# Gated mix of an S4 convolution and a GeGLU: another form of the block convolution, and a shorter gelu, last tile and mix in the feed-forward part

## Chip, cores and metric

The kernel runs on one core of one Trainium2 chip. The metric is the device time of one execution in microseconds (us), lower is better. A profile is one further execution recorded by the hardware profiler; "span" is what it covers, from the first to the last recorded instruction.

## What is computed

The input x is 2048 tokens of 640 channels in bf16. A state-space layer gives every channel a filter of 2048 taps, and the causal convolution of x with it is one branch; a GeGLU feed-forward layer is the other. A gate per token mixes them.

```
K[d,l] = Re( sum_n C[d,n] * exp(dt[d]*A[d,n]*l) * dt[d]*B[d,n] )        # 640 x 2048, n = 128
a = causal_conv(x, K) + x * Dskip                                        # over the 2048 tokens
b = ( gelu_tanh(x @ w_gate) * (x @ w_up) ) @ w_down                      # 640 -> 1728 -> 640
g = sigmoid( sum(x * gate_w) )                                           # one number per token
out = g * a + (1 - g) * b
```

## The kernel before, in words

The program runs in four stages, one after the other in the source. The instructions of each engine stand in an order that the framework's scheduler makes from the source order and the dependencies; buffers are taken from pools, and a pool that is opened after another one was closed lies on the same memory, so that its first writers wait for the last users of the old one.

1. *Filter generation* (lines 103 to 314). For ten blocks of 64 channels it makes tables of exponentials and sines and contracts them on PE. The result K_sb holds the filter with 128 tokens on the partitions. The change leaves this stage as it is.

2. *Convolution* (lines 321 to 426). The 2048 tokens are cut into four blocks of 512 (NB = 4), and the transform has length T = 1024. All four blocks of x are loaded at once into u_sb, which is a_sb itself (L332). Half-integer frequencies need 512 real and 512 imaginary parts and no special Nyquist row, so that a spectrum is two parts (q) of four tiles (ft) of 128 frequencies. The tables FK, FU and FI are made in twelve wide steps: two tensor_scalar operations make the phase as an integer whose lower 16 bits wrap by themselves (L357), and one Sin takes 1024 columns at once (L359). fwd_block (L364) transforms a block: 64 matmuls of 320 columns, each group of eight evicted by a Scalar copy (L375). The filter's blocks get another table than the input's, and combine (L377) joins neighbouring filter blocks beforehand, so that the product of spectra needs no correction for wrap-around later. products(c) (L385) multiplies and adds spectra on Vector with operations 2560 columns wide. inverse(c) (L402) transforms back on PE, 16 matmuls per output tile of 128 tokens, and adds x * Dskip while it evicts (L412, L413).

3. *Gate and up projections* (L441 to L494). x is loaded again, transposed (xT, five transposing loads), then the weights Wg, Wu, Wd and the gate vector gwc, all from SP's queue. The gate logits are 80 small matmuls into a PSUM tile of their own (L458). Then there are 14 hidden tiles (13 of 128 and one of 64) times four stretches of 512 tokens. For each, five matmuls make the gate part pGt and five the up part pUt. Scalar copies both to bf16 (Gs, Us); Vector builds the gelu's polynomial in three operations, Scalar takes a sigmoid, and Vector multiplies twice (L484 to L494). The result is HT.

4. *Down projection and mix* (L496 to L513). For each of 16 tiles of 128 tokens 28 matmuls (14 of 512 and 14 of 128 columns) fill pD, which has one buffer. Scalar copies it to b_sb, Vector subtracts and mixes in two operations, and SP stores the tile.

Lines that the steps of the prediction touch: L338 to L360 (tables), L364 to L375 (forward), L377 to L383 (combine), L385 to L400 (products), L402 to L416 (inverse), L443 to L453 (loads of the feed-forward part), L455 to L462 (gate), L474 to L494 (gate and up), L497 to L513 (down).

Of the kernel before, what the change touches and what calls it, by code (L numbers as in the profile page):

```python
# [9 lines left out]
ALU = mybir.AluOpType  # L10
ACT = mybir.ActivationFunctionType
FP32 = mybir.dt.float32
BF16 = mybir.dt.bfloat16
I32 = mybir.dt.int32
# [8 lines left out]
def kernel(  # L23
# [19 lines left out]
    nc = tc.nc  # L43
# [279 lines left out]
    with ExitStack() as k2:  # L323
        big = k2.enter_context(tc.tile_pool(name="spec", bufs=1))
        wk = k2.enter_context(tc.tile_pool(name="cwork", bufs=2))
        psT = k2.enter_context(tc.tile_pool(name="pstf", bufs=2, space=bass.MemoryType.PSUM))
        psY = k2.enter_context(tc.tile_pool(name="psinv", bufs=2, space=bass.MemoryType.PSUM))
        DH = D // 2
        NF = 4
        I16 = mybir.dt.int16  # L330

        u_sb = a_sb  # L332
        for c in range(NB):
            nc.sync.dma_start(out=u_sb[:, 4 * c:4 * c + 4, :],
                              in_=u2[c * S:(c + 1) * S, :].rearrange("(t p) d -> p t d", p=128))

        odd_i = big.tile([128, 512], I32, name="odd_i")
        nc.gpsimd.iota(odd_i[:], pattern=[[2, 512]], base=1, channel_multiplier=0)  # L338
        oddf = big.tile([128, 512], FP32, name="oddf")
        nc.vector.tensor_copy(out=oddf[:], in_=odd_i[:])  # L340
        FU = big.tile([128, 4, 2, 512], BF16, name="FU")
        FK = big.tile([128, 4, 2, 512], BF16, name="FK")
        FI = big.tile([128, NF, 2, 512], BF16, name="FI")
        scl = big.tile([128, 12], FP32, name="scl")
        for a in range(4):
            nc.vector.tensor_scalar(out=scl[:, a:a + 1], in0=row_f[:], scalar1=32.0, scalar2=16.0 * (256 * a + 1),
                                    op0=ALU.mult, op1=ALU.add)
            nc.vector.tensor_scalar(out=scl[:, 4 + a:5 + a], in0=row_f[:], scalar1=32.0, scalar2=32.0 * 128 * a,
                                    op0=ALU.mult, op1=ALU.add)
            f0 = 256 * (a // 2) + a % 2  # L350
            nc.vector.tensor_scalar(out=scl[:, 8 + a:9 + a], in0=row_f[:], scalar1=64.0, scalar2=16.0 * (2 * f0 + 1),
                                    op0=ALU.mult, op1=ALU.add)
        for tab, s0 in ((FK, 4), (FU, 0), (FI, 8)):
            for a in range(4):
                ph = wk.tile([128, 2, 512], I32, name="ph")
                for q in range(2):
                    nc.vector.tensor_scalar(out=ph[:, q, :], in0=oddf[:], scalar1=scl[:, s0 + a:s0 + a + 1],  # L357
                                            scalar2=(16384.0 if q == 0 else 0.0), op0=ALU.mult, op1=ALU.add)
                nc.scalar.activation(out=tab[:, a, :, :], in_=ph[:].bitcast(I16)[:, :, 0:1024:2], func=ACT.Sin,  # L359
                                     scale=TWO_PI * FUDGE / 65536.0)  # L360

        Uf = big.tile([128, NB, 2, NF, D], BF16, name="Uf")
        Kf = big.tile([128, NB, 2, NF, D], BF16, name="Kf")

        def fwd_block(tab, src, b, spec):
            for ft in range(NF):
                f0 = 256 * (ft // 2) + ft % 2
                for q in range(2):
                    pU = psT.tile([128, 2, 512], FP32, name="pU")
                    for h in range(2):  # L370
                        for k in range(4):
                            nc.tensor.matmul(pU[:, h, 0:DH], lhsT=tab[:, k, q, f0:min(512, f0 + 256):2],  # L372
                                             rhs=src[:, 4 * b + k, h * DH:(h + 1) * DH],
                                             start=(k == 0), stop=(k == 3))
                    nc.scalar.copy(out=spec[:, b, q, ft, :].rearrange("p (h d) -> p h d", h=2), in_=pU[:, :, 0:DH])  # L375

        def combine(m):  # L377
            for ft in range(NF):
                odd = ft % 2 == 1
                nc.vector.tensor_tensor(out=Kf[:, m, 0, ft, :], in0=Kf[:, m, 0, ft, :], in1=Kf[:, m - 1, 1, ft, :],  # L380
                                        op=(ALU.subtract if odd else ALU.add))
                nc.vector.tensor_tensor(out=Kf[:, m, 1, ft, :], in0=Kf[:, m, 1, ft, :], in1=Kf[:, m - 1, 0, ft, :],
                                        op=(ALU.add if odd else ALU.subtract))  # L383

        def products(c):  # L385
            M = wk.tile([128, 2, NF, D], BF16, name="M")
            for i in range(c + 1):
                Ur, Ui = Uf[:, i, 0, :, :], Uf[:, i, 1, :, :]
                Kr, Ki = Kf[:, c - i, 0, :, :], Kf[:, c - i, 1, :, :]
                for q, (k0, k1, op1) in enumerate(((Kr, Ki, ALU.subtract), (Ki, Kr, ALU.add))):  # L390
                    if i == 0:
                        nc.vector.tensor_tensor(out=M[:, q], in0=Ur, in1=k0, op=ALU.mult)
                    else:
                        t0 = wk.tile([128, NF, D], BF16, name="t0")
                        nc.vector.tensor_tensor(out=t0[:], in0=Ur, in1=k0, op=ALU.mult)
                        nc.vector.tensor_tensor(out=M[:, q], in0=M[:, q], in1=t0[:], op=ALU.add)  # L396
                    t1 = wk.tile([128, NF, D], BF16, name="t1")
                    nc.vector.tensor_tensor(out=t1[:], in0=Ui, in1=k1, op=ALU.mult)
                    nc.vector.tensor_tensor(out=M[:, q], in0=M[:, q], in1=t1[:], op=op1)  # L399
            return M  # L400

        def inverse(c, M):  # L402
            for mo in range(4):
                pY = psY.tile([128, 2, 512], FP32, name="pY")
                for h in range(2):
                    for q in range(2):
                        for ft in range(NF):
                            nc.tensor.matmul(pY[:, h, 0:DH], lhsT=FI[:, ft, q, 128 * mo:128 * mo + 128],  # L408
                                             rhs=M[:, q, ft, h * DH:(h + 1) * DH],
                                             start=(q == 0 and ft == 0), stop=(q == 1 and ft == NF - 1))  # L410
                t = 4 * c + mo
                nc.vector.tensor_tensor(out=u_sb[:, t, :], in0=u_sb[:, t, :], in1=dsk[:], op=ALU.mult)  # L412
                nc.vector.scalar_tensor_tensor(out=a_sb[:, t, :].rearrange("p (h d) -> p h d", h=2),  # L413
                                               in0=pY[:, :, 0:DH], scalar=2.0 / T,
                                               in1=u_sb[:, t, :].rearrange("p (h d) -> p h d", h=2),
                                               op0=ALU.mult, op1=ALU.add)  # L416

        for b in range(NB):
            fwd_block(FK, K_sb, b, Kf)
        for c in range(NB):  # L420
            fwd_block(FU, u_sb, c, Uf)
        for m in range(NB - 1, 0, -1):
            combine(m)
        for c in range(NB):
            M = products(c)
            inverse(c, M)
# [3 lines left out]
    dchs = [(0, 512), (512, D - 512)]  # L430
    with ExitStack() as k3:
# [3 lines left out]
        psC = k3.enter_context(tc.tile_pool(name="psconst", bufs=1, space=bass.MemoryType.PSUM))  # L435
# [19 lines left out]
        pG = psC.tile([128, TC], FP32, name="pgate")  # L455
# [5 lines left out]
        nc.scalar.copy(out=glog[:], in_=pG[:])  # L461
# [5 lines left out]

        HT = fp.tile([128, nft, L], BF16, name="HT")
        GELU_C = 2.0 * math.sqrt(2.0 / math.pi)
        for ft in range(nft):  # L470
            fsz = 128 if ft < nft_full else f_last
            f0 = ft * 128
            for tq in range(L // 512):
                toks = slice(tq * 512, (tq + 1) * 512)  # L474
                pGt = psF.tile([128, 512], FP32, name="pGt")
                pUt = psF.tile([128, 512], FP32, name="pUt")
                for kt in range(nkt):
                    nc.tensor.matmul(pGt[:fsz, :], lhsT=Wg[:, kt, f0:f0 + fsz], rhs=xT[:, kt, toks],  # L478
                                     start=(kt == 0), stop=(kt == nkt - 1))
                for kt in range(nkt):  # L480
                    nc.tensor.matmul(pUt[:fsz, :], lhsT=Wu[:, kt, f0:f0 + fsz], rhs=xT[:, kt, toks],  # L481
                                     start=(kt == 0), stop=(kt == nkt - 1))
# [13 lines left out]
        for tt in range(TC):  # L496
# [9 lines left out]
            if "b" in dbg:  # L506
                nc.sync.dma_start(out=dbg["b"][toks, :], in_=b_sb[:])
# [37 lines left out]
```

## Time and profile before

| | us |
|---|---|
| median of 3 runs (776.99 to 779.27) | 777.49 |
| the profiled execution, its own time | 777.49 |
| its span | 775.7 |
| PE busy (64% of the span) | 494.7 |
| Vector busy (75%) | 579.3 |
| Scalar busy (58%) | 446.6 |
| GpSimd busy (1%) | 6.3 |

"PE" is the matrix engine and "PEld" its weight loads, DVE is Vector, ACT Scalar, POOL GpSimd, and SP the engine that issues the loads and stores. The page cuts the span into 40 equal slices of 19.4 us and gives the busy share of each in tenths; these rows show the stages one after the other:

```profile
PE   0036656566658556435899963306199999998886
...
DVE  5978899889998998866157999994068787773333
ACT  1129999999999999984766400000077766751111
...
PEclk9999697798698689666999995757599999999999
```

The first 18 slices are filter generation (Scalar and Vector near full), then come the transforms (PE), the products (Vector alone), one slice and a bit with no engine at work, the gate and up projections and the down projection (PE). "PEclk" is the PE clock that was granted, in tenths of full speed. In the rows of groups that are quoted further down, the numbers behind the bar are total busy us, mean ns of one, and the idle time of the engine just before with what ended it. In timelines the columns are start and length in us, engine, line, operation, and in brackets the idle time before it and its releaser.

### The profile page before, as it was taken

To read this page: it belongs to the slowest core of one execution; us is meant where nothing else is said; L and a number is where in the kernel's file an instruction comes from. 1 tells how busy PE (TensorE), PEld (TensorE's weight loads), DVE (VectorE), ACT (ScalarE), POOL (GpSimd) and SP (SyncE) were. 2 spreads that over 40 slices of the span, in tenths; PEclk is the share of its full clock that TensorE was granted. 3 is DMA by queue.
4 is the path that set the end of the run, shared out by engine and by line. 5 is a ranking of instruction groups with operands and counts; after the bars stand their busy time and mean duration, and the time that the engine had idled before them with its cause. 6 is when DMAs were issued, how large, how long until landed. Compare 5 with 4: busy or idle time off the path is not lost.

```text
span 775.7 us, 8859 instructions
## 1 busy us (share of the span) xinstructions
PE 494.7 (64%) x3518; PEld 259.9 (34%) x3556; DVE 579.3 (75%) x906; ACT 446.6 (58%) x492; POOL 6.3 (1%) x26
## 2 busy tenths in 40 slices
PE   0036656566658556435899963306199999998886
PEld 0012223233224222133577641203044444444443
DVE  5978899889998998866157999994068787773333
ACT  1129999999999999984766400000077766751111
POOL 2000000000000000000000000000000000000000
PEclk9999697798698689666999995757599999999999
DMA  3000000000000000060000000001940000000000
GB/s 68 0 0 0 1 1 15 0 14 14 1 15 14 1 14 14 0 164 14 1 1 1 2 0 0 1 0 33 282 165 1 1 0 1 1 10 26 35 35 35
DMA packets 44650, 19.01 MB, mean 25 GB/s; under 512 B 37248, under 2 KB 43328, under 8 KB 44608
## 3 DMA queue, kind: packets, MB, share of 16 engines
q1 hardware_dynamic: 44608, 18.44, 9.4%
q8 instruction: 28, 0.46, 0.3%
q14 instruction: 14, 0.11, 0.1%
HBM read 9.91 MB, written 2.62 MB: 16 GB/s over the span
## 4 chain that ended last, share of the span: by engine, by line
ACT 40%; DVE 31%; PE 23%; SPq 3%; issue 2%; DMA 2%; ACTq 0%; DVEq 0%
PE pD L502 8%; PE pU L372 5%; ACT sg L492 4%; DVE M L399 3%; DVE sg L493 3%; DVE q L490 3%; DVE M L396 2%; DVE HT L494 2%; PE pY L408 2%; SPq L443 2%; ACT L249 2%; DVE q L488 2%; ACT L266 1%; ACT b_sb L505 1%; DVE q L489 1%
## 5 line engine op out<-in xcount | busy, mean ns | idle before, releaser
L484 ACT CAST Gs<-pGt 128x512 bf16<-128x512 f32 (+1 forms) x56 | 32.3, 577 | 124.8 <-PE pGt L478 124.4
L257 DVE TENSOR_SCALAR kM<-pph 128x512 f32<-128x512 f32 x120 | 79.6, 682 | 22.3 <-PE pph L253 14.5
L478 PE MATMUL pGt<-xT,Wg 128*128 128x512 bf16 (+1 forms) x269 | 69.8, 384 | 25.2 <-DMA Wg<-in_B_w_gate_dram 22.1
L408 PE MATMUL pY<-M,FI 128*128 128x320 bf16 x256 | 42.1, 329 | 57.5 <-DVE M L399 55.1
L502 PE MATMUL pD<-Wd,HT 128*128 128x128 bf16 (+3 forms) x440 | 68.0, 298 | 12.8 <-ACT b_sb L505 12.4
L481 PE MATMUL pUt<-xT,Wu 128*128 128x512 bf16 (+1 forms) x280 | 69.2, 379 | 0.4 <-ACT Us L486 0.4
L492 ACT ACTIVATE sg<-q 128x512 bf16<-128x512 bf16 (+1 forms) x56 | 35.2, 630 | 35.6 <-DVE q L490 35.3
L408 PEld LDWEIGHTS <-FI 128*128 128x128 bf16 x256 | 27.1, 106 | 72.3 <-DVE M L399 51.2
L509 DVE TENSOR_TENSOR diff<-a_sb,b_sb 128x640 f32<-128x640 bf16 x16 | 13.2, 825 | 50.1 <-ACT b_sb L505 50.1
L502 PEld LDWEIGHTS <-HT 128*128 128x128 bf16 x448 | 34.8, 97 | 46.3 <-issue 22.0
L505 ACT CAST b_sb<-pD 128x640 bf16<-128x640 f32 x16 | 11.0, 691 | 66.1 <-PE pD L502 66.1
L478 PEld LDWEIGHTS <-Wg 128*128 128x128 bf16 (+1 forms) x280 | 27.6, 99 | 60.3 <-issue 30.2
L372 PE MATMUL pU<-K_sb,FK 128*128 128x320 bf16 x256 | 38.8, 313 | 11.7 <-ACT FK L359 8.8
L488 DVE TENSOR_TENSOR q<-Gs 128x512 bf16<-128x512 bf16 (+1 forms) x56 | 23.4, 418 | 26.6 <-ACT Gs L484 26.6
L493 DVE TENSOR_TENSOR sg<-sg,Gs 128x512 bf16<-128x512 bf16 (+1 forms) x56 | 23.8, 424 | 21.1 <-ACT sg L492 20.4
L481 PEld LDWEIGHTS <-Wu 128*128 128x128 bf16 (+1 forms) x280 | 27.6, 99 | 33.4 <-issue 0.7
L253 PE MATMUL pph<-RX_1_104,b_bf 128*128 128x512 bf16 x40 | 19.1, 486 | 29.7 <-DVE p_2486 L258 7.3
L253 PE MATMUL pph<-RX_0_103,b_bf 128*128 128x512 bf16 x40 | 17.3, 437 | 30.7 <-DVE p_1655 L258 6.4
L372 PE MATMUL pU<-a_sb,FU 128*128 128x320 bf16 x256 | 34.9, 299 | 0.0
L372 PEld LDWEIGHTS <-FK 128*128 128x128 bf16 x256 | 25.5, 101 | 24.8 <-ACT FK L359 10.7
L486 ACT CAST Us<-pUt 128x512 bf16<-128x512 f32 (+1 forms) x56 | 32.5, 582 | 1.3 <-PE pUt L481 1.3
L375 ACT CAST Uf<-pU 128x640 bf16<-128x640 f32 x32 | 22.1, 692 | 12.6 <-PE pU L372 12.6
(383 smaller groups left out, 1219.5 us busy)
## 6 DMA issues: line engine op xcount, KB each, us to landing
a_sb<-in_A_u_dram SPq DMA_DIRECT2D x4, 640.0 KB, 5.5
out_dram<-o_sb SPq DMA_DIRECT2D x16, 160.0 KB, 1.8
Wg<-in_B_w_gate_dram SPq DMA_DIRECT2D x1, 2160.0 KB, 8.7
Wu<-in_B_w_up_dram SPq DMA_DIRECT2D x1, 2160.0 KB, 13.5
Wd<-in_B_w_down_dram SPq DMA_DIRECT2D x1, 2080.0 KB, 19.5
K_sb<-K_671 SPq DMA_DIRECT2D x4, 64.0 KB, 2.3
K_sb<-K_948 SPq DMA_DIRECT2D x4, 64.0 KB, 2.5
K_sb<-K_1225 SPq DMA_DIRECT2D x4, 64.0 KB, 2.2
```

The costliest lines, as they stand in the source:

```text
L253: nc.tensor.matmul(pph[:], lhsT=lhs_b, rhs=rhs_rx, start=True, stop=True)
L257: nc.vector.tensor_scalar(out=kM[:], in0=tau_src, scalar1=MAGIC, scalar2=None, op0=ALU.add)
L372: nc.tensor.matmul(pU[:, h, 0:DH], lhsT=tab[:, k, q, f0:min(512, f0 + 256):2], rhs=src[:, 4 * b + k, h * DH:(h + 1) * DH], start=(k == 0), ...
L408: nc.tensor.matmul(pY[:, h, 0:DH], lhsT=FI[:, ft, q, 128 * mo:128 * mo + 128], rhs=M[:, q, ft, h * DH:(h + 1) * DH], start=(q == 0 and ft ...
L478: nc.tensor.matmul(pGt[:fsz, :], lhsT=Wg[:, kt, f0:f0 + fsz], rhs=xT[:, kt, toks], start=(kt == 0), stop=(kt == nkt - 1))
L481: nc.tensor.matmul(pUt[:fsz, :], lhsT=Wu[:, kt, f0:f0 + fsz], rhs=xT[:, kt, toks], start=(kt == 0), stop=(kt == nkt - 1))
L484: nc.scalar.copy(out=Gs[:fsz], in_=pGt[:fsz])
L486: nc.scalar.copy(out=Us[:fsz], in_=pUt[:fsz])
L488: nc.vector.tensor_tensor(out=q[:fsz], in0=Gs[:fsz], in1=Gs[:fsz], op=ALU.mult)
L492: nc.scalar.activation(out=sg[:fsz], in_=q[:fsz], func=ACT.Sigmoid, scale=GELU_C)
L493: nc.vector.tensor_tensor(out=sg[:fsz], in0=sg[:fsz], in1=Gs[:fsz], op=ALU.mult)
L502: nc.tensor.matmul(pD[:, d0:d0 + dn], lhsT=HT[:fsz, ft, toks], rhs=Wd[:fsz, ft, d0:d0 + dn], start=(ft == 0), stop=(ft == nft - 1))
```

## The change

Both halves of the program behind filter generation are exchanged.

*Convolution.* The half-integer form gives way to one with whole frequencies 0 to 512: nine tiles of 128 rows (NT = 9), real and imaginary parts in turn, the ninth holding only the Nyquist row. One forward table FW serves filter and input. FW and FI are built in 72 tiles of 128x128: each takes six or seven Vector operations, with the phase reduced to the nearest whole turn by adding and subtracting a large constant, and a Sin. The input is loaded block by block into ub, a pool of two buffers that is opened after the tables' work pool was closed; x * Dskip is put into a_sb beforehand. The products are operations on single tiles of 640 columns. There is no combine; a step Mc = Sc + sgn * Sprev joins the sums of two successive blocks instead. The transforms' matmuls are split at 512 columns: 512 and 128.

*Feed-forward part.* The gelu is one Scalar function read straight from PSUM, and one Vector operation multiplies it with the up part in PSUM. The last half tiles of gate and up share one group of matmuls through a joined weight tile Wl, which GpSimd copies together. The gate logits use a buffer of pGt. pD has two halves of 320 columns and two buffers; Scalar forms g * a ahead of time (ga), and one Vector operation adds (1 - g) * pD.

The diff, cut to its core:

```diff
+        FW = big.tile([128, 4, NT, 128], BF16, name="FW")
+        FI = big.tile([128, NT, 4, 128], BF16, name="FI")
...
+        dw = dctx.enter_context(tc.tile_pool(name="dftwork", bufs=2))
+
+        def angle_negfrac(dst_pt, v_in, shape):
...
+            nc.vector.tensor_scalar(out=tv, in0=v_in, scalar1=1.0 / T, scalar2=None, op0=ALU.mult)
...
+            nc.vector.tensor_scalar(out=kv, in0=tv, scalar1=MAGIC, scalar2=None, op0=ALU.add)
+            nc.vector.scalar_tensor_tensor(out=dst_pt, in0=kv, scalar=-MAGIC, in1=tv, op0=ALU.add, op1=ALU.subtract)
+
+        for kind in range(2):
+            for a in range(4):
...
+                for mt in range(NT):
+                    dst = FW[:, a, mt, :] if kind == 0 else FI[:, mt, a, :]
...
+                    if kind == 0:
+                        nc.vector.tensor_scalar(out=fv[:], in0=col_f[:], scalar1=float(128 * tt), scalar2=None, op0=ALU.add)
+                        nc.vector.tensor_tensor(out=v[:], in0=fv[:], in1=s_val[:].to_broadcast([128, 128]), op=ALU.mult)
...
+                    nc.vector.tensor_scalar(out=v[:], in0=v[:], scalar1=off, scalar2=None, op0=ALU.add)
+                    nfq = dw.tile([128, 128], FP32, name="nfq")
+                    angle_negfrac(nfq[:], v[:], [128, 128])
+                    if kind == 0:
+                        nc.scalar.activation(out=dst, in_=nfq[:], func=ACT.Sin, scale=sin_scale)
+                    else:
+                        tmp = dw.tile([128, 128], FP32, name="sinv")
+                        nc.scalar.activation(out=tmp[:], in_=nfq[:], func=ACT.Sin, scale=sin_scale)
+                        nc.vector.tensor_scalar(out=dst, in0=tmp[:], scalar1=2.0 / T, scalar2=None, op0=ALU.mult)
...
+        def fwd_block(src, kidx, spec, b):
+            for mt in range(NT):
+                pU = psT.tile([128, D], FP32, name="pU")
+                for (d0, dn) in dchs:
+                    for k in range(4):
+                        nc.tensor.matmul(pU[:, d0:d0 + dn], lhsT=FW[:, k, mt, :], rhs=src[:, kidx(k), d0:d0 + dn],
+                                         start=(k == 0), stop=(k == 3))
+                nc.scalar.copy(out=spec[:, b, mt, :], in_=pU[:])
...
+            ub = upool.tile([128, 4, D], BF16, name="ub")
+            nc.sync.dma_start(out=ub[:], in_=u2[c * S:(c + 1) * S, :].rearrange("(t p) d -> p t d", p=128))
+            for k in range(4):
+                nc.vector.tensor_tensor(out=a_sb[:, 4 * c + k, :], in0=ub[:, k, :], in1=dsk[:], op=ALU.mult)
+            fwd_block(ub, lambda k: k, Uf, c)
...
+                        nc.vector.tensor_tensor(out=tmp[:], in0=Ur, in1=Kr, op=ALU.mult)
+                        nc.vector.tensor_tensor(out=Sr, in0=Sr, in1=tmp[:], op=ALU.add)
...
+                    nc.vector.scalar_tensor_tensor(out=Mc[:, mt, :], in0=Sprev[:, mt, :],
+                                                   scalar=sgn[:], in1=Sc[:, mt, :],
+                                                   op0=ALU.mult, op1=ALU.add)
...
+                    for kt in range(NT):
+                        nc.tensor.matmul(pY[:, d0:d0 + dn], lhsT=FI[:, kt, mo, :], rhs=Mc[:, kt, d0:d0 + dn],
+                                         start=(kt == 0), stop=(kt == NT - 1))
+                tcx = 4 * c + mo
+                nc.vector.tensor_tensor(out=a_sb[:, tcx, :], in0=a_sb[:, tcx, :], in1=pY[:], op=ALU.add)
...
-        pG = psC.tile([128, TC], FP32, name="pgate")
+        pG = psF.tile([128, 512], FP32, name="pGt")
...
-                nc.scalar.copy(out=Gs[:fsz], in_=pGt[:fsz])
...
-                nc.scalar.copy(out=Us[:fsz], in_=pUt[:fsz])
...
-                nc.scalar.activation(out=sg[:fsz], in_=q[:fsz], func=ACT.Sigmoid, scale=GELU_C)
...
+                    nc.scalar.activation(out=Gs[:], in_=pGt[:], func=ACT.Gelu_apprx_tanh)
+                    nc.vector.tensor_tensor(out=HT[:, ft, toks], in0=pUt[:], in1=Gs[:], op=ALU.mult)
+                else:
+                    for kt in range(nkt):
+                        nc.tensor.matmul(pGt[:], lhsT=Wl[:, kt, :], rhs=xT[:, kt, toks],
+                                         start=(kt == 0), stop=(kt == nkt - 1))
...
-            pD = psF.tile([128, D], FP32, name="pD", bufs=1)
...
+            nc.scalar.activation(out=ga[:], in_=a_sb[:, tt, :], func=ACT.Copy, scale=gf[:, tt:tt + 1])
+            pD = psD.tile([128, 2, 512], FP32, name="pD")
+            for h in range(2):
...
-            nc.scalar.copy(out=b_sb[:], in_=pD[:])
...
-            nc.vector.tensor_tensor(out=diff[:], in0=a_sb[:, tt, :], in1=b_sb[:], op=ALU.subtract)
...
+            nc.vector.scalar_tensor_tensor(out=o_sb[:].rearrange("p (h d) -> p h d", h=2), in0=pD[:, :, 0:DH],
+                                           scalar=omg[:, tt:tt + 1],
+                                           in1=ga[:].rearrange("p (h d) -> p h d", h=2),
                                            op0=ALU.mult, op1=ALU.add)
```

## The prediction

> **What bounds the kernel now.** I first read the busy times of stretches that I cut at the stage borders (columns: PE, weight loads, Vector, Scalar, GpSimd busy, granted PE clock, DMA share, GB/s), then the timeline at the borders and in one period of each loop, then the rows of single groups for prices.
>
> ```profile
> 354.90:404.00 49.10, 38.61 (x256) 25.58 (x257) 18.13 (x54) 32.64 (x43) 0.00 (x0) 0.90 0.04 6
> 412.50:538.50 126.00, 68.36 (x451) 45.92 (x449) 118.93 (x104) 17.33 (x26) 0.00 (x0) 0.77 0.00 0
> 538.50:560.40 21.90, 0.00 (x0) 0.00 (x0) 0.71 (x1) 0.00 (x0) 0.00 (x0) 0.60 0.95 241
> 560.40:689.70 129.30, 125.68 (x630) 57.33 (x641) 99.76 (x270) 89.29 (x167) 0.00 (x0) 0.99 0.09 32
> 689.70:775.70 86.00, 68.00 (x441) 34.75 (x448) 31.11 (x43) 13.31 (x21) 0.00 (x0) 1.00 0.09 31
> ```
>
> Filter generation ends on Vector at 354.9. Tables and the transform of K follow (PE), then the products until 538.5 (Vector busy 119 of 126 us), a pure load, gate and up matmuls (PE 126 of 129), and the down projection (PE 68 of 86).
>
> ```profile
> 515.42 1.49 DVE L395 TENSOR_TENSOR t_4142<-Uf,Kf 128x2560 bf16<-128x2560 bf16 x1
> 516.82 1.49 DVE L399 TENSOR_TENSOR M<-M,t_4139 128x2560 bf16<-128x2560 bf16 x1
> ...
> 528.58 9.76 PE L408 MATMUL pY<-M,FI 128*128 128x320 bf16 x56 [2.29 <-DVE M L399]
> 538.38 0.82 DVE L413 SCALAR_TENSOR_TENSOR a_sb<-pY,a_sb 128x640 bf16<-128x640 f32 x1 [1.35 <-PE pY L408]
> 538.49 13.00 SPq L443 DMA_TRANSPOSE xT<-in_A_u_dram  x5
> ```
>
> Wide products start every 1.40 us though each lasts 1.49, also where one needs the result of the op before last: neighbours overlap by 0.09. The load of xT starts when the last inverse transform ends.
>
> ```profile
> 601.18 1.24 PE L478 MATMUL pGt<-xT,Wg 128*128 128x512 bf16 x5
> 602.26 1.24 PE L481 MATMUL pUt<-xT,Wu 128*128 128x512 bf16 x5
> ...
> 705.02 4.28 PE L502 MATMUL pD<-Wd,HT 128*128 128x512 bf16 x28 [0.82 <-ACT b_sb L505]
> 709.37 0.69 ACT L505 CAST b_sb<-pD 128x640 bf16<-128x640 f32 x1 [4.41 <-PE pD L502]
> 710.12 4.28 PE L502 MATMUL pD<-Wd,HT 128*128 128x512 bf16 x27 [0.82 <-ACT b_sb L505]
> ```
>
> Five matmuls of 512 columns take 1.08 us, 0.216 each, without a break: gate and up stand at PE's pace, the gelu chain is hidden. Down is not: a tile takes 5.10 us, PE waits for the eviction of its only pD.
>
> ```profile
> L380 DVE TENSOR_TENSOR Kf<-Kf 128x640 bf16<-128x640 bf16 x12 | 5.3, 487 | 24.9 <-ACT Kf L375 24.9
> 27.57 0.82 DVE L162 TENSOR_TENSOR r_149<-vr 128x640 f32<-128x640 f32 x1
> 43.24 0.49 DVE L181 TENSOR_SCALAR u2t<-u2t 128x640 f32<-128x640 f32 x1
> 355.18 0.13 DVE L346 TENSOR_SCALAR scl<-row_f 128x1 f32<-128x1 f32 x1
> ```
>
> These are the prices for the new small Vector operations.
>
> **What the Trainium skill says.** "VectorE: DVE Perf Modes", section "The perf-mode tier table": tensor_tensor runs at 2x in bf16 and 1x in fp32, tensor_scalar at 2x in fp32. The trace agrees: 487 ns against 820 at 640 elements, and 490 for the fp32 tensor_scalar. The table has no row for scalar_tensor_tensor. Same page, section on the TRN2 errata: each SBUF-source instruction pays a fixed extra, so many small tiles pay it often; here 4 x 0.403 = 1.61 us for what one 1.40 us operation did. "TensorE: Matmul & The Clock Gate", Part 1: after about 3.4 us idle the array runs at half clock until as long busy. Agrees: after the 22 us load, five matmuls took 2.5 us (0.43 apart) before 0.216. "ScalarE: Activation LUTs", "What ACT_TABLE_LOAD costs": all functions cost the same per element, so gelu from PSUM should cost what the copy Gs does (577 ns); a load is given at 1283 ns, and the trace has 1283.
>
> **Tables and K transform** (354.9 to 404 now). Twelve wide Sin calls go. Vector gets 476 operations for FW and FI. A 128x128 fp32 tensor_scalar: 0.13 + 128/640 x (0.49 - 0.13) = 0.20 us, 0.13 apart with overlap; tensor_tensor or scalar_tensor_tensor likewise 0.28, 0.20 apart. The built program's order interleaves two tiles, so each needs the op before last, as in the products. Unlike there the operations are short; bounds: 0.13/0.20 apart, or full duration plus the 0.04 seen between dependent ones (0.24/0.32). I take the lower. An FW tile: 4 x 0.13 + 2 x 0.20 = 0.92; 32 of them and some 2 us of small ones: 31.4, to 386.3. FI adds a tiny one per tile: 32 x 0.99 + 4 = 35.7, to 422. None of it precedes 354.9: in the order all of it stands behind the last K0 copy, and up to there both programs are alike on PE, Vector and Scalar.
>
> PE's first group needs FW of all four k: 354.9 + 0.75 x 31.4 + 2 + 0.3 (Sin) = 380.7. A group is 4 x 0.216 plus four of 128 columns at (4.28 - 0.15 - 14 x 0.216)/14 = 0.08: 1.18. 36 groups are 42.5, cold start 2, to 425. Scalar holds the evictions (0.69) and FI's Sins in one order; each can wait for the other, 3 us more: 428. The loads of ub wait for FI's last Vector and Scalar instruction (their buffers lie where the work tiles were), though they are issued on SP with nothing else behind but each other. They land 5.5 us later (as a_sb now): 433.5. Two cold groups and an eviction, 4.4 + 0.7: products can start at 438.6, against 412.6 now.
>
> **Products.** Removed: 72 wide operations x 1.40 = 101 us; the combines were hidden behind PE. Added: 304 of 128x640, (487 ns less the 0.085 overlap = 0.403) = 122.5; 27 Mc steps, bounds 0.403 (2x) and 0.737 (1x, as L413, which however reads PSUM), taken at 0.737 = 19.9; 16 additions from pY at 0.737 = 11.8, as many as now; 8 of the u x dsk multiplies (the other 8 stand ahead) 3.2. Sum 157.4, less the last four additions behind the tail: 154.5. Behind Mc of c = 0, 1, 2 Vector waits about 1, 1 and 2 us for the first inverse; what is queued behind these waits is the next block's products. PE's own work, 36 more forward groups (42.5) and 16 inverse tiles of 18 x 0.148 = 2.66, is 85 of these 160 us and hidden. Vector's last Mc: 438.6 + 154.5 + 4 = 597.1. Two interleaved inverses end 1.9 later, two more 5.3, cold clock 2: xT's load can start at 606.3 instead of 538.5: **+67.8**.
>
> **Gate and up.** Load and landings keep their distances. In the order PE now does only 10 pUt matmuls, then the 80 gate ones, which need gwc, the last load; it landed 34.4 us behind xT's first issue (572.9). Now PE had done 52 matmuls by then. So from 576.1 (old clock) 560 - 20 merged - 10 = 530 x 0.216 = 114.5 remain, to 690.6; gelu's two table loads hold up the third pGt 1.5, cold start 1: 693.1 against 689.7, **+3.4**. The removed 2 Scalar and 4 Vector operations a tile were hidden: 0. One gelu (0.58) and one multiply from PSUM (0.68) per 2.16 us are covered by PE. Wl's two GpSimd copies are needed 100 us later: 0, and some 2 us if not.
>
> **Down.** 448 matmuls of 320 columns at 0.136 (pU now: 37.12 us for 272) = 61.1; two pD hide eviction and mix (0.88 and a Scalar scaling of 0.7 against 3.8 a tile). Tail: one mix 0.9, output 2.65; now a copy and a subtraction stand ahead of it. 61.1 + 3.6 = 64.7 instead of 86.0: **-21.3**.
>
> Sum: 67.8 + 3.4 - 21.3 = +49.9; span 775.7 becomes 825.6. The profiled execution took 777.49, 1.8 more than its span, and is the median of the three: **827 us**.
>
> **Rivals.** *Latency-paced tables.* If the short operations don't overlap, FW takes 32 x 1.60 + 3 = 54 and FI 32 x 1.77 + 6 = 63; FI ends at 472, 44 later: **871**. For it: no pair of such short dependent operations in the trace. Against: the overlap is the same 0.08 at 128x1 (0.06 apart at 0.13) and at 2560. *Cheaper combine.* Mc at 0.403 saves 9.0 and no coupling 3: **815**. *Feed-forward under the products.* PE idles about 75 us during the products. If xT and the weights did not wait for the convolution's buffers, the 22 us load and those 75 us of matmuls would vanish beneath Vector: 827 - 22 - 75 = **730**; from 50 us hidden on, the change is not slower. Against: in the built program xT's first transpose waits for the last inverse matmul, and PE's order has the pUt matmuls behind it.
>
> **Chances.** Forecast with its bounds (cheaper combine, partial coupling, a denser down stage at a lower clock) 808 to 848: 0.78, in it the cheaper combine with 0.15. Tables paced in part or wholly by latency, 848 to 880: 0.15. Feed-forward under the products: 0.04, of which 0.01 within 0.3%. Below 808 but slower: 0.03. The range takes half of the second case: 808 to 858. About 0.3% is what a measurement of this kernel can tell from no change.
>
> **What would show it.** Right: FI's last operation near 428, Vector without gaps from 439 to 597 at 0.40 per product, xT near 606, down at 3.8 a tile. Wrong: table operations over 0.2 apart, Mc at 0.4, products starved by Uf, or matmuls of L478's kind before the last pY.

## The result and the profile after

The changed kernel takes 821.57 us (median of 4 runs, 820.38 to 823.02); beside it the kernel before took 777.24. The ratio is 1.0567, with a 95% interval of 1.0539 to 1.0595: slower, inside the range of 808 to 858 that was forecast, and 5.4 us below the predicted 827.0. The span is 818.6 us where 825.6 was forecast.

The head of the page of the changed kernel, with the same rows as were shown of before (slices of 20.5 us):

```profile
span 818.6 us, 9462 instructions
...
PE   0045636655765673334979990500504999999998
...
DVE  5979898899998988699979999999800333333212
...
PEclk9999779688977986665999996655665999999999
```

Vector's row tells most of it: behind filter generation it is near full from the eighteenth to the twenty-ninth slice, through tables and products, where before it was so for some six slices, the products alone. The busy times of stretches, cut at the new stage borders (columns as in the prediction):

```profile
354.90:432.50 77.60, 46.94 (x294) 25.08 (x301) 73.05 (x481) 41.39 (x109) 0.00 (x0) 0.81 0.08 21
432.50:588.50 156.00, 76.39 (x499) 40.59 (x508) 155.95 (x352) 24.22 (x35) 0.00 (x0) 0.75 0.03 9
588.50:622.50 34.00, 6.59 (x55) 4.00 (x56) 3.20 (x4) 0.00 (x0) 0.64 (x2) 0.67 0.76 220
622.50:747.30 124.80, 121.83 (x611) 55.74 (x623) 37.62 (x56) 36.95 (x61) 0.26 (x1) 0.97 0.05 15
747.30:818.60 71.30, 67.63 (x448) 40.92 (x446) 15.53 (x18) 12.32 (x16) 0.00 (x0) 1.00 0.11 38
```

Tables, the transform of K and that of the first input tiles take 77.6 us up to the first product (57.7 before). In the products Vector is busy 155.95 of 156.0 us: nothing makes it wait, and PE's 76 us lie beneath. Then come the last inverse and the load, then PE at work in the gate and up projections and in the down projection.

The timeline of the changed kernel at the start of the products, and at the end of the convolution (weight loads and other rows left out):

```profile
424.94 0.93 SPq L416 DMA_DIRECT2D ub<-in_A_u_dram  x2
...
429.27 4.92 PE L403 MATMUL pU<-ub,FW 128*128 128x512 bf16 x21 [4.29 <-DMA ub<-in_A_u_dram]
...
432.49 0.48 DVE L433 TENSOR_TENSOR Sc<-Uf,Kf 128x640 bf16<-128x640 bf16 x1
...
432.89 0.48 DVE L436 TENSOR_TENSOR Sc<-Uf,Kf 128x640 bf16<-128x640 bf16 x1
...
582.01 6.48 DVE L461 SCALAR_TENSOR_TENSOR Mc<-Sc,sgn 128x640 bf16<-128x640 bf16 x8
...
595.43 0.82 DVE L473 TENSOR_TENSOR a_sb<-a_sb,pY 128x640 bf16<-128x640 bf16 x1 [1.62 <-PE pY L470]
595.53 2.39 SPq L490 DMA_TRANSPOSE xT<-in_A_u_dram  x1
```

The load of the input ub starts at 424.94, right behind the last Sin of the tables on Scalar (424.61 to 424.91), and lands 4.3 us later. Products start 0.40 apart. The eight last Mc steps take 6.48 us, 0.80 each. xT's load starts at 595.53; before it was 538.49.

The start of the gate and up projections in the changed kernel:

```profile
622.50 4.43 PE L535 MATMUL pUt<-xT,Wu 128*128 128x512 bf16 x10 [27.11 <-DMA Wu<-in_B_w_up_dram]
629.13 2.15 PE L505 MATMUL pGt<-gwc,xT 128*128 128x1 bf16 x80 [2.19 <-DMA gwc<-in_gate_w_dram]
...
631.51 4.74 PE L532 MATMUL pGt<-xT,Wg 128*128 128x512 bf16 x14 [0.24 <-issue]
...
636.09 1.24 PE L535 MATMUL pUt<-xT,Wu 128*128 128x512 bf16 x5
637.07 0.58 ACT L537 ACTIVATE Gs<-pGt 128x512 bf16<-128x512 f32 x1
637.17 1.24 PE L532 MATMUL pGt<-xT,Wg 128*128 128x512 bf16 x5
```

PE waits for Wu, does ten matmuls, waits for gwc, does the gate, and only then starts the first gate tile; from there groups of five stand 1.08 apart to the end. A stretch of the down projection:

```profile
797.73 1.85 PEld L556 LDWEIGHTS <-HT 64*128 64x128 bf16 x14 [0.26 <-issue]
798.14 0.89 DVE L559 SCALAR_TENSOR_TENSOR o_sb<-pD,omg,ga 128x640 bf16<-128x640 f32 x1 [3.34 <-PE pD L556]
...
799.85 1.85 PEld L556 LDWEIGHTS <-HT 64*128 64x128 bf16 x14 [0.27 <-issue]
801.96 0.09 PEld L556 LDWEIGHTS <-HT 64*128 64x128 bf16 x1 [0.26 <-issue]
```

PE's matmuls run here without a gap in their row, but the row of the weight loads stops for 0.26 us once in each chain of 14, at the tile of 64 rows: a chain takes 2.11 us (797.73, 799.85, 801.96), where 14 matmuls at the 0.1365 us of the prediction are 1.91.

### The profile page after: what moved, and what is told of

Read it like the earlier page. It is cut to its first block, busy times and chain, and to the rows that moved or that the text cites. A ratio compares the mean times of both kernels' runs of the same rounds, so it can differ in the third digit from the quotient of the medians.

```text
span 818.6 us, 9462 instructions
## 1 busy us (share of the span) xinstructions
PE 502.3 (61%) x3585; PEld 255.8 (31%) x3632; DVE 593.0 (72%) x1342; ACT 403.3 (49%) x449; POOL 6.7 (1%) x27
## 4 chain that ended last, share of the span: by engine, by line
DVE 31%; PE 31%; ACT 30%; SPq 4%; issue 2%; DMA 2%; DVEq 0%; ACTq 0%
PE pD L556 8%; PE pGt L532 7%; PE pUt L535 7%; DVE Mc L461 3%; PE pY L470 2%; ACT L249 2%; SPq L490 2%; DVE nfq L343 1%; ACT L266 1%; SPq L498 1%; ACT L254 1%; DVE ptmp L440 1%; DVE Sc L445 1%; DVE ptmp L444 1%; DVE ptmp L442 1%
## 5 line engine op out<-in xcount | busy, mean ns | idle before, releaser
L538 DVE TENSOR_TENSOR HT<-pUt,Gs 128x512 bf16<-128x512 f32 x52 | 36.0, 692 | 74.6 <-PE pUt L535 71.6
L470 PE MATMUL pY<-Mc,FI 128*128 128x128 bf16 (+1 forms) x211 | 36.6, 323 | 78.9 <-DVE Mc L461 78.3
L535 PE MATMUL pUt<-xT,Wu 128*128 128x512 bf16 x260 | 66.6, 389 | 27.1 <-DMA Wu<-in_B_w_up_dram 27.1
L403 PEld LDWEIGHTS <-FW 128*128 128x128 bf16 x576 | 46.5, 101 | 70.6 <-ACT FW L385 27.0
L537 ACT ACTIVATE Gs<-pGt 128x512 bf16<-128x512 f32 x52 | 31.0, 597 | 75.9 <-PE pGt L532 75.9
L556 PE MATMUL pD<-Wd,HT 128*128 128x320 bf16 x448 | 67.8, 301 | 0.0
L532 PE MATMUL pGt<-xT,Wg 128*128 128x512 bf16 x249 | 65.1, 386 | 0.8 <-issue 0.2
L403 PE MATMUL pU<-K_sb,FW 128*128 128x128 bf16 (+1 forms) x282 | 43.7, 311 | 28.1 <-ACT FW L385 25.3
L405 ACT CAST Uf<-pU 128x640 bf16<-128x640 f32 x36 | 24.9, 692 | 42.9 <-PE pU L403 42.9
L403 PE MATMUL pU<-ub,FW 128*128 128x128 bf16 (+1 forms) x284 | 42.7, 306 | 4.6 <-DMA ub<-in_A_u_dram 4.3
L535 PEld LDWEIGHTS <-Wu 128*128 128x128 bf16 x260 | 25.8, 99 | 59.0 <-issue 29.5
```

Source lines behind the costliest of these rows:

```text
L403: nc.tensor.matmul(pU[:, d0:d0 + dn], lhsT=FW[:, k, mt, :], rhs=src[:, kidx(k), d0:d0 + dn], start=(k == 0), stop=(k == 3))
L405: nc.scalar.copy(out=spec[:, b, mt, :], in_=pU[:])
L470: nc.tensor.matmul(pY[:, d0:d0 + dn], lhsT=FI[:, kt, mo, :], rhs=Mc[:, kt, d0:d0 + dn], start=(kt == 0), stop=(kt == NT - 1))
L532: nc.tensor.matmul(pGt[:], lhsT=Wg[:, kt, f0:f0 + 128], rhs=xT[:, kt, toks], start=(kt == 0), stop=(kt == nkt - 1))
L535: nc.tensor.matmul(pUt[:], lhsT=Wu[:, kt, f0:f0 + 128], rhs=xT[:, kt, toks], start=(kt == 0), stop=(kt == nkt - 1))
L537: nc.scalar.activation(out=Gs[:], in_=pGt[:], func=ACT.Gelu_apprx_tanh)
```

## Where the time went

The start of xT's load and the first down matmul divide the span in three (three down matmuls are done ahead, at 745.08; the border stands where the stage would start with them):

| part | before | after | difference | predicted |
|---|---|---|---|---|
| up to xT's load | 538.5 | 595.5 | +57.0 | +67.8 |
| to the down stage | 151.2 | 151.8 | +0.6 | +3.4 |
| down stage | 86.0 | 71.3 | -14.7 | -21.3 |
| span | 775.7 | 818.6 | +42.9 | +49.9 |

Within the convolution: the first product starts at 432.5 instead of 412.6 (+19.9), from there to the end of Vector's last step before the last inverse it is 156.0 instead of 115.9 us (+40.1), and from that to xT's load 7.0 instead of 10.0 (-3.0).

The +40.1 can be worked out from the pitches in the traces (an estimate): 288 short products at 0.403 for 72 wide ones at 1.40 are +15, the 16 operations for the Nyquist row +6, the 27 steps Mc at 0.80 +22, and five fewer multiplications by Dskip in this stretch -2, together 41.

## The experiments

The theory was the prediction's: the convolution costs by the number of short Vector operations, the forward table stands bare ahead of PE, the inverse table lies beneath PE, and the down stage gains by its second buffer. Rivals stand with each run. The kernel before gave 777.08, 776.72 and 777.16 us beside the three sets of four experiments.

**The new feed-forward part alone**, behind the convolution of before.

> The old convolution with the new feed-forward part. Theory (the two halves add up, since the second starts only when the first has ended): the new feed-forward part took 818.6 - 595.5 = 223.1 us from the first transposed load to the end, the old one 775.7 - 538.5 = 237.2, so 14 us less than before: about 763 us. Rival (the halves interact, or the gain of the new part is larger than it looks and eaten by something in the changed convolution): clearly under 755, or no gain at all.

Measured: 763.40 us, ratio 0.9817 (0.9792 to 0.9842), span 761.4.

**The new convolution alone**, ahead of the feed-forward part of before.

> The new convolution with the old feed-forward part. Theory (additive): xT's load starts 595.5 - 538.5 = 57 us later, all else as before: about 834 us. Rival (interaction): more than 4 us away from that.

Measured: 834.08 us, ratio 1.0734 (1.0713 to 1.0756), span 831.4; xT's load starts at 594.7. The two halves add: -13.7 and +57.0 are +43.3, and the whole change is +44.3. The change is one loss and one smaller gain that hardly touch each other; neither rival came true.

**The gelu alone**, in the kernel before, with the gate logits in a buffer of their own as before.

```diff
-                nc.scalar.copy(out=Gs[:fsz], in_=pGt[:fsz])
...
-                nc.vector.tensor_tensor(out=HT[:fsz, ft, toks], in0=sg[:fsz], in1=Us[:fsz], op=ALU.mult)
+                nc.scalar.activation(out=Gs[:fsz], in_=pGt[:fsz], func=ACT.Gelu_apprx_tanh)
+                nc.vector.tensor_tensor(out=HT[:fsz, ft, toks], in0=pUt[:fsz], in1=Gs[:fsz], op=ALU.mult)
```

> The kernel before with only the gelu exchanged: one Scalar gelu from PSUM and one Vector multiply with the up part in PSUM, also for the 64-row tile; gate, down projection and mix as before. Theory (PE sets the pace of gate and up, the removed four Vector and two Scalar operations a tile were hidden): only PE's short waits for Scalar and the wait for the last tile's chain can go, 2.7 us and about 1 us: 773 to 777 us. Rival (the elementwise chain is a bound of its own): 10 us or more less, under 767.

Measured: 771.98 us, ratio 0.9937 (0.9921 to 0.9953). From xT's load to the first down matmul it is now 146.9 us (537.1 to 684.0), 4.3 less than before. The time is 1 us under the 773 to 777 of the theory, and far from the rival's 767. The prediction had called the removed gelu operations hidden, at nothing. They were not quite. The timeline of the kernel before has these stops of PE, two of ten:

```profile
623.49 1.24 PE L478 MATMUL pGt<-xT,Wg 128*128 128x512 bf16 x5 [0.23 <-ACT Gs L484]
630.36 1.24 PE L478 MATMUL pGt<-xT,Wg 128*128 128x512 bf16 x4 [0.23 <-ACT Gs L484]
```

They lie 6.87 us apart, where six groups at 1.08 take 6.48: a stop costs 0.39, and ten 3.9 us. The trace without the old gelu has none of these ten; PE waits there for Gs once, 0.34 us, at the start of the stage.

**The down projection and mix alone**, in the kernel before. To make room for the second pD, the gate logits go into a buffer of pGt, as in the changed kernel.

```diff
-        pG = psC.tile([128, TC], FP32, name="pgate")
+        pG = psF.tile([128, 512], FP32, name="pGt")
...
-            pD = psF.tile([128, D], FP32, name="pD", bufs=1)
+            ga = fwk.tile([128, D], FP32, name="ga")
+            nc.scalar.activation(out=ga[:], in_=a_sb[:, tt, :], func=ACT.Copy, scale=gf[:, tt:tt + 1])
+            pD = psF.tile([128, 2, 512], FP32, name="pD")
```

> The kernel before with only the down projection and mix exchanged (two pD of two halves of 320 columns, g*a formed on Scalar, one mixing operation); to make room in PSUM the gate logits use a buffer of pGt, as in the changed kernel. Theory: down costs 4.2 us a tile instead of 5.1, 14.7 us less with the shorter end; the gate in pGt lets PE do only 20 matmuls before gwc lands instead of 52, which costs (116.5 us of matmuls from 576 on) some 3 us: about 765 us. Rival (the gate's place costs nothing): 762; rival (the down gain comes from the gelu's relief of Scalar): near 777.

Measured: 769.64 us, ratio 0.9901 (0.9883 to 0.9919), 4.6 us worse than expected. The down stage gained what it should (767.1 less 695.5, the first down matmul of 695.77 with two done ahead, is 71.6 us; before 86.0). The rest was lost in the stage ahead: xT's load to the first down matmul now took 157.7 us (537.8 to 695.5) instead of 151.2. So the rival in which the gate's place costs nothing is out, and so is the one in which the down gain comes from the new gelu. The edit in that stage is the place of the gate logits, with the small operations for the mix beside it; 0.9 us of the 6.5 is a stop of PE at two down matmuls that stand early in its order (578.93). With the prices of these runs the new feed-forward part is -14.4 for down, -4.3 for the gelu, -4.3 for 20 merged matmuls at 0.216 (worked out; no run has the merged tile alone), and +6.5 or more for the gate in pGt. A run further down undoes that last one.

**Wide products** in the changed kernel:

```diff
-                for t in range(4):
-                    Ur = Uf[:, i, 2 * t, :]
...
-                    tmp = wk.tile([128, D], BF16, name="ptmp")
+                Ur = Uf[:, i, 0:8:2, :]
+                Ui = Uf[:, i, 1:8:2, :]
...
+                tmp = wk.tile([128, 4, D], BF16, name="ptmp")
```

> The changed kernel with only the products exchanged: each multiplies or adds the four tiles of a spectrum part at once (2560 columns, 72 operations, before 288 of 640). Theory: four short operations take 4 x 0.403 = 1.61 us, a wide one 1.40, so 72 x 0.21 = 15 us go; but the first product of block 0 must now wait for eight transformed tiles instead of two, about 6 x 1.09 = 6.5 us, so 9 us less: about 813. Rival: Vector is not what sets the end of the products (PE or the waits for the inverse do); then there is no gain, 820 to 822.

Measured: 816.36 us, ratio 1.0514 (1.0486 to 1.0543). This is 5 us below the changed kernel, but the intervals of the two ratios just touch, so the trace has to carry it. In the timeline of this kernel, Vector's rows:

```profile
439.79 1.49 DVE L432 TENSOR_TENSOR Sc<-Uf,Kf 128x2560 bf16<-128x2560 bf16 x1 [6.86 <-ACT Uf L405]
441.20 1.49 DVE L433 TENSOR_TENSOR ptmp<-Uf,Kf 128x2560 bf16<-128x2560 bf16 x1
...
576.63 4.85 DVE L460 SCALAR_TENSOR_TENSOR Mc<-Sc,sgn 128x640 bf16<-128x640 bf16 x6
```

Vector now waits 6.86 us for the transform of the whole first block, so products start 7.3 us later than in the changed kernel. They end at 581.5 instead of 588.5: 141.7 us instead of 156.0, 14.3 less where 15 was worked out. The tail behind the last Mc is 9.1 us instead of 7.0, so that 4.9 us are left at xT's load (590.6). The theory holds in the place it speaks of, and the rival is out; its sum left out the longer tail, and had the start 0.8 us too early.

**A plain addition for Mc** in the changed kernel:

```diff
-                    nc.vector.scalar_tensor_tensor(out=Mc[:, mt, :], in0=Sprev[:, mt, :],
-                                                   scalar=sgn[:], in1=Sc[:, mt, :],
-                                                   op0=ALU.mult, op1=ALU.add)
+                    nc.vector.tensor_tensor(out=Mc[:, mt, :], in0=Sprev[:, mt, :], in1=Sc[:, mt, :], op=ALU.add)
```

> The changed kernel with the step Mc as a plain tensor_tensor addition of the two sums; the sign of each frequency row is left out. Theory: scalar_tensor_tensor has no fast mode for bf16, and its 27 runs at 0.80 us are on Vector's path; a plain addition starts every 0.40, so 27 x 0.40 = 10.7 us go: about 811. Rival: the pace of the Mc steps is set by the wait for their inputs, or they lie beside the inverse transform on PE: less than 3 us, 819 to 822.

Measured: 813.80 us, ratio 1.0469 (1.0449 to 1.0488). The rows of groups, first of the changed kernel, then of this one (total busy, mean ns, idle before):

```profile
L461 DVE SCALAR_TENSOR_TENSOR Mc<-Sc,sgn 128x640 bf16<-128x640 bf16 x27 | 21.9, 891 | 0.0
L445 DVE TENSOR_TENSOR Sc<-Sc,ptmp 128x640 bf16<-128x640 bf16 x24 | 11.3, 496 | 0.0
```

```profile
L461 DVE TENSOR_TENSOR Mc<-Sc 128x640 bf16<-128x640 bf16 x27 | 11.1, 474 | 0.0
L445 DVE TENSOR_TENSOR Sc<-Sc,ptmp 128x640 bf16<-128x640 bf16 x24 | 11.1, 474 | 0.0
```

The same sum of two bf16 tiles takes 474 ns as a tensor_tensor and 891 as a scalar_tensor_tensor. The last Mc ends 11.0 us earlier, as worked out; 2.4 us of it come back in the tail (9.47 us instead of 7.04): PE's last inverse now starts 3.2 us ahead of the end of the Mc steps, and in the changed kernel 6.7 us. The rival, that this lies beside PE, is refuted but for these 2.4 us, which the theory had left out. The Trainium skill, "VectorE: DVE Perf Modes", section "The perf-mode tier table", lists tensor_tensor at 2x in bf16, which the trace confirms, and has no row for scalar_tensor_tensor; here it took even longer than the fp32 operations of the same size (820 ns).

**No inverse table**, and **no forward table**, in the changed kernel. Each replaces one of the two loops by a constant fill:

```diff
+        nc.vector.memset(FI[:], 0.001)
-        for kind in range(2):
+        for kind in range(1):
```

> The changed kernel without the making of the inverse table FI (one memset in its place, so that the inverse transform multiplies by a constant). Theory: Vector makes FI beneath PE's transform of K, which ends at about 424 us whether FI is there or not; only the late load of the first block's input goes, 4 to 6 us: 816 to 818. Rival: all of the table work stands on the path, since Vector does it all: 38 us less, about 783.

Measured: 817.75 us, ratio 1.0516 (1.0492 to 1.0539); the first product is at 429.37 instead of 432.49. The interval just touches that of the changed kernel, so here too the trace has to carry it.

> The changed kernel without the making of the forward table FW (one memset in its place, so that the forward transforms multiply by a constant). Theory: FW is what PE's transform of K waits for. PE starts about 24 us earlier and ends near 400; FI ends at about 394, the input lands at 398, the products start near 403 instead of 432: about 29 us less, 792. Rival: PE's transform is paced by something else (K's own casts or the clock), then less than 20 us go, over 801.

Measured: 795.04 us, ratio 1.0235 (1.0214 to 1.0257); the first product is at 405.90. The two tables take about the same Vector time (31.6 us to 386.5, then 38.6 to 425.1), but leaving FI out shortens the kernel by 3 to 4 us, and leaving FW out by 26.5. The rivals, 38 us for FI and less than 20 for FW, are both out. The timeline of the kernel without FI:

```profile
357.05 3.90 DVE L345 MEMSET FI<- 128x4608 bf16 x1 [0.91 <-issue]
...
360.89 0.34 DVE L377 TENSOR_SCALAR fv<-col_f 128x128 f32<-128x128 f32 x2
...
387.57 7.01 PE L404 MATMUL pU<-K_sb,FW 128*128 128x512 bf16 x42 [7.10 <-ACT FW L386]
...
427.35 2.98 PE L404 MATMUL pU<-ub,FW 128*128 128x512 bf16 x19
...
428.64 0.69 ACT L406 CAST Uf<-pU 128x640 bf16<-128x640 f32 x1 [0.39 <-PE pU L404]
429.37 0.49 DVE L434 TENSOR_TENSOR Sc<-Uf,Kf 128x640 bf16<-128x640 bf16 x1 [27.56 <-ACT Uf L406]
```

PE goes from K's last groups to the input's first without a gap, Scalar waits for PE, and Vector has stood idle for 27.6 us: the path is PE behind FW, and most of FI lay in Vector's idle time.

The 3 to 4 us are too small a price for FI, though. The constant fill that stands in for it holds Vector for 3.9 us ahead of FW, with 0.9 us idle before it, and filter generation ended 1.8 us later in this execution, so that PE's transform of K starts at 387.57, where it started at 380.89 in the changed kernel. From there to the first product it is 41.8 us without FI and 51.6 us with it: FI costs 9.8 us on the path (3.8 us of the medians and 4.8 for the fill are 8.6). Of these, 4.3 are the load of the input, which is issued only when FI is done, and 2.4 are stops of PE for Scalar's copies of Kf (2.6 us in eight stops with FI, 0.2 in one without). That the measured time fell into the expected 816 to 818 was luck: the theory had left out the stops, the fill and the later start, which go opposite ways. Without FW the fill does no such harm, since PE starts there only when K_sb has landed (358.78).

**The last hidden tile filled up to 128 rows**, on the kernel with the old convolution and the new feed-forward part:

```diff
+            nc.gpsimd.memset(Wd[f_last:128, nft_full, :], 0.0)
...
+        nc.gpsimd.memset(HT[f_last:128, nft_full, :], 0.0)
...
-                    fsz = 128 if ft < nft_full else f_last
+                    fsz = 128
```

> The convolution before with the new feed-forward part (763.4), and the last hidden tile of HT and Wd filled with zeros from 64 to 128 rows, so that each down matmul contracts 128 rows. Theory: each of the 32 chains loses 0.2 us at its one weight load of 64 rows; 32 x 0.2 = 6.4 us go, a chain of 14 takes 1.91 instead of 2.11 us: about 757. Rival: the 0.2 us belong to the change from one chain to the next, not to the 64 rows; then 763.

Measured: 757.90 us, ratio 0.9759 (0.9732 to 0.9786). The timeline of this kernel in the down stage:

```profile
739.77 6.41 PE L510 MATMUL pD<-Wd,HT 128*128 128x320 bf16 x46
739.91 6.08 PEld L510 LDWEIGHTS <-HT 128*128 128x128 bf16 x45
741.38 0.88 DVE L513 SCALAR_TENSOR_TENSOR o_sb<-pD,omg,ga 128x640 bf16<-128x640 f32 x1 [2.92 <-PE pD L510]
...
745.19 0.88 DVE L513 SCALAR_TENSOR_TENSOR o_sb<-pD,omg,ga 128x640 bf16<-128x640 f32 x1 [2.92 <-PE pD L510]
```

45 weight loads follow each other without a stop, across three chains, and a tile takes 3.81 us instead of 4.22: 16 x 0.41 = 6.6 us. The rival, that the stop belongs to the change of chains, is refuted, since the chains still change. In this execution 2.1 us of that were lost again in the stage ahead (153.5 us against 151.4), about half of it where the gate tiles start, as the first 14 matmuls took 5.88 us (4.86 without the edit). Why is not shown. The medians differ by 5.5, and by 6.9 where the next edit is in place as well (755.29 and 748.35).

**The gate logits in a buffer of pD**, on the same kernel:

```diff
-        pG = psF.tile([128, 512], FP32, name="pGt")
+        pG = psD.tile([128, 2, 512], FP32, name="pD")
```

> The convolution before with the new feed-forward part (763.4), the gate logits in a buffer of pD instead of pGt. Theory: what the faster gelu and the merged tile won in the gate and up stage was lost because the gate's 80 matmuls in pGt hold up every gate tile until gwc, the last load, has landed. In this kernel PE's order is that of before again (20 gate, 20 up matmuls first). With the gelu alone the stage took 146.9 us from xT's first load to the first down matmul; less 20 merged matmuls x 0.216 that is 142.6, against 151.3: about 8.5 us less, 755. Rival: the stage is bound elsewhere (table loads, landing of Wu); within 2 us of 763.

Measured: 755.29 us, ratio 0.9716 (0.9697 to 0.9736). PE's timeline at the start of the stage, first without this edit, then with it:

```profile
565.40 2.29 PE L487 MATMUL pUt<-xT,Wu 128*128 128x512 bf16 x5 [26.87 <-DMA Wu<-in_B_w_up_dram]
...
571.78 2.14 PE L457 MATMUL pGt<-gwc,xT 128*128 128x1 bf16 x80 [1.96 <-DMA gwc<-in_gate_w_dram]
```

```profile
560.30 2.29 PE L484 MATMUL pGt<-xT,Wg 128*128 128x512 bf16 x5 [21.29 <-DMA Wg<-in_B_w_gate_dram]
562.81 4.11 PE L484 MATMUL pGt<-xT,Wg 128*128 128x512 bf16 x14 [0.22 <-issue]
566.76 4.48 PE L487 MATMUL pUt<-xT,Wu 128*128 128x512 bf16 x20
...
573.88 2.14 PE L457 MATMUL pD<-gwc,xT 128*128 128x1 bf16 x80
```

PE starts when Wg has landed, 21.3 us idle instead of 26.9, and does 53 matmuls before it comes to the gate at 573.88, 1.3 us after gwc has landed (issued at 563.99, 8.6 us in flight). From xT's load to the first down matmul it is 142.1 us instead of 151.4, so the rival is out; the span falls by 8.9 us (761.4 to 752.5) and the median by 8.1, for one line and the indices that go with it. What the gate cost in pGt was not its 80 matmuls but its place in a pool of two, ahead of every gate tile, and its need of the last load. With 9.3 us for it in place of 6.5 (with the old gelu PE had 20 up matmuls to do ahead of the gate, with the new one ten), the prices above add to -13.7, which is what the new feed-forward part alone had measured.

**Both edits.**

> Both of the last two edits: filled last hidden tile and the gate logits in pD, with the convolution before. Theory: they act in different stages and add, 6.4 + 8.5 = 15 us: about 748. Rival: the down stage, once dense, is held by something else (Vector's mix of 0.88, the stores), then more than 751.

Measured: 748.35 us, ratio 0.9620 (0.9596 to 0.9645): they add (15 us below the 763.40), and this version beats both kernels.

**The matmuls split at 512 and 128 columns with two buffers of pD.**

```diff
-            pD = psD.tile([128, 2, 512], FP32, name="pD")
-            for h in range(2):
+            pD = psD.tile([128, D], FP32, name="pD")
+            for (d0, dn) in [(0, 512), (512, D - 512)]:
```

> The convolution before with the new feed-forward part (763.4), the down matmuls split at 512 and 128 columns as before, with the two buffers of pD kept. Theory: the down stage gains by the second buffer, not by the split in two halves: 14 x 0.216 + 14 x 0.056 + 0.4 is 4.2 us a tile, as with halves of 320: 763 to 764. Rival: the halves matter (short matmuls of 128 columns wait for their weight loads): a tile takes 4.4 us or more, 767 or more.

Measured: 763.83 us, ratio 0.9824 (0.9798 to 0.9851), against 0.9817 (0.9792 to 0.9842) with two halves. The even halves are worth nothing by themselves. What is left is the second buffer together with the shorter mix, and no run has one without the other. The wait for the only pD, 0.82 us a tile in the trace of before or some 12 us in all, is what went.

## Why the prediction came out right, step by step

| step | predicted | measured |
|---|---|---|
| FW done on Vector | 386.3 | 386.5 |
| FI done on Vector | 428 | 425.1 |
| first product | 438.6 | 432.5 |
| last Mc done | 597.1 | 588.5 |
| xT's load starts | 606.3 | 595.5 |

*The sign and the cause hold.* The tables' short operations stand at their lower bound (a pair of table operations every 0.27 or 0.4 us; Vector waits only once, 0.38 us, before the last), so the rival of latency-paced tables, 871, is refuted. The feed-forward part did not move under the products. The rival of the cheaper combine, 815, had Mc at 0.403: it ran at 0.80 each, even above the upper bound of 0.737, so its 27 steps cost 21.7 us and not 19.9.

*The nearness of the sum is in part luck.* The convolution was forecast 10.8 us too long, gate and up 2.8 too long, and the down stage 6.6 too short, so that 7.0 us are left of misses of 20 in all.

*The forward table and K's transform.* FW's end was right to 0.2 us and so was the start of K's transform on PE (380.9 for 380.7), and the run without FW shows that FW is what PE waited for. FI lies beneath PE but for some 9 us. The first product came 6.1 us earlier than forecast in small terms: FI's end (2.9), the input landed 4.1 us behind it and not 5.5 (1.4), and 3.3 us from its landing to the first product, not 5.1 (1.8). The first of these is no proof that Scalar's evictions and FI's Sins did not hold each other up. PE did stop for 2.6 us, close to the 3 that were put for this, and FI took Vector 38.6 us and not 35.7. But the groups of K's transform were shorter (next paragraph, 36 x 0.09 = 3.2 us), so that the transform, its stops included, ended at 425.0, where the prediction had it without them.

*A step whose working was wrong though its result did little.* I took 0.08 us for a matmul of 128 columns, as the remainder of a down tile of before. That remainder held the stops at the tile of 64 rows. A group of K's transform took 1.09 us and not 1.18, and (1.09 - 4 x 0.216)/4 is 0.056. The Trainium skill, "TensorE: Matmul & The Clock Gate", section "Back-to-back issue gap", has a formula for the isolated gap that gives an estimate of 55.8 ns for 128 columns; the trace agrees, although its matmuls form a stream with a weight load each, for which the same section gives about 81 ns.

*Products.* 158.5 us forecast, 156.0 measured. The pitch of 0.40 was right, Mc cost 1.8 more, and the 4 us of waits for the first inverse of three blocks did not occur: Vector is busy 155.95 of 156.0. The tail was 7.0 us instead of 9.2, since the inverse runs along with the Mc steps.

*Gate and up.* The mechanism was right: PE's gate matmuls waited for gwc, and 530 matmuls at 0.216 followed. The size was 2.8 us too large: the matmuls behind the gate started 36.0 us after xT's first issue and not 37.6, and what came on top of the 530 took 1.3 and not 2.5. "Hidden: 0" for the gelu was off by 4.3 us, as a run showed. It did no harm to the sum, since 530 x 0.216 has no such stops in it; the gain was lost again to the gate's place in pGt. The prediction's reading of the slow start of before was a little short: it was seven matmuls 0.43 apart, 3.0 us (560.42 to 563.39), and not five.

*Down.* This is the single term that failed most: 64.7 forecast, 71.3 measured. "448 matmuls of 320 columns at 0.136" holds for 416 of them. At the 32 of 64 rows the weight load waits, 0.2 us each, 32 x 0.2 = 6.4. The trace of before had it in sight, as a stop of the weight loads at the tile of 64 rows, and I took the price from pU, where every tile is full:

```profile
707.91 0.09 PEld L502 LDWEIGHTS <-HT 64*128 64x128 bf16 x1 [0.42 <-issue]
```

## What to carry to other kernels

Of two tables of like cost, the one that the next engine waits for counts nearly in full, and the other far less (here 26.5 us against some 9): look at who is idle while it is made. When a part is left out to price it, look whether what stands in for it lies on the path itself. A small job that shares a rotating PSUM buffer with the main loop takes a place in the main loop's order, and with it the wait for its own late input; a buffer that is idle at that time is the better place. Take the price of a loop's odd last tile from that tile, not from the full ones.

## What I had not expected of the hardware

- A chain of 14 matmuls of 320 columns that ends in a tile of 64 rows loses 0.2 us there, although the 64-row weight load itself takes 93 ns and a full one 98. Filled with zeros to 128 rows the stop is gone. Why the load waits is not shown by these runs.
- scalar_tensor_tensor on bf16 tiles of 128x640 in SBUF takes 0.89 us on average (0.80 apart), as against 0.47 (0.40 apart) for a tensor_tensor: a multiply by a sign that looks free in the code doubles the step.
- Removing Vector work just ahead of PE's last inverse gave back about 2 us of it in the tail (2.1 and 2.4), in both runs that did so: in the changed kernel PE's last inverse starts 6.7 us ahead of the last Mc's end, and in these two 3.1 and 3.2 us.
